# A third buffer for the low parts of q and k, taken from GpSimd's descriptor ring

## The chip, the core and the metric

The kernel runs on one core of a Trainium2 chip. The metric is the device time of one execution in microseconds (us), the median of several executions. The engines that matter are TensorE (PE, matmuls), VectorE (DVE), ScalarE (ACT), GpSimd (POOL) and SyncE (SP), which here only issues DMAs. Every engine has its own queue and works through it strictly in that order: an instruction that waits holds up all that stands behind it on its engine.

## What is computed

Causal attention over 8 batches, 8 heads, 576 tokens and head width 64, with a bias from a running sum; then a two-dimensional Fourier transform of the 512-wide tokens, added to them; then a layer norm and a two-layer MLP (512 to 2048 to 512). Cut to what matters:

```python
cum = np.cumsum(np.maximum(s, 0.0), axis=-1)
bias = -(cum[:, :, :, None] - cum[:, :, None, :])
scores = scale * np.matmul(q, k.transpose(0, 1, 3, 2))
scores = np.where(causal, -1e9, scores + np.minimum(bias, 0.0))
attn = np.exp(scores - scores.max(-1, keepdims=True))
attn = attn / (attn.sum(-1, keepdims=True) + 1e-09)
x = np.matmul(attn, v)                     # heads side by side: 8 x 576 x 512
u = x + np.real(np.fft.fft(np.fft.fft(x, axis=1), axis=2))
un = (u - mean(u)) / np.sqrt(var(u) + 1e-06)
out = u + np.maximum(un @ w_ch1, 0.0) @ w_ch2
```

## The kernel before

Attention goes by pairs of heads: 8 batches of 4 pairs make 32 pairs, and the main loop has 32 passes. Products are made in a reduced format in which a number is kept as a high part and a low part; three products of such parts stand for one exact one.

Pass i does these things side by side: `scores(i)` (L488, L489: the products of q and k for pair i, high parts from the tile KQ, low parts from q1 and k1; L492: the exponential on ACT into P), `maxes(i + 1)` (L456: products pm of the high parts; L463 on DVE: their row maxima into Mx; L468: Mx transposed on PE as pmt; L470 and L471: ACT copies it to mt and a DMA writes it into a row of KQ that scores(i + 1) reads), `low(i + 1)`, `high(i + 2)` (L415, L417: ACT copies q and k into KQ, one copy for each head) and `av(i - 1)` (L520: P times v). From pass 6 on, in every fourth pass and the one after it, `folds` runs on DVE, ACT and POOL (L250 to L265: Aw, Df, De, Do, e, eh, the even and odd halves that the Fourier products need), and `fourier` follows on PE (L283 to L314). MLP weights are converted beside it (L82 to L88). After pass 31 the MLP runs over all tokens.

`low(i)` is the part that the change touches. For a pair it issues two DMAs (L427, L428) that copy the high parts beside the low ones, two subtractions on DVE (L432, one for each head: k minus its high part, into k1) and two on POOL (L435, the same for q, into q1). q1 and k1 have two buffers, one in the pool `att` and one in the pool `atop`, by turns, so that pair i writes where pair i - 2 was read; scores(i - 2) ends with pass i - 2, and L432 of pair i stands at the start of pass i - 1.

KQ has three tiles (`NR = 3`, tile i % 3 for pair i), and the loaded inputs qk three buffers. The PE's order is written by hand (`weave` mixes the streams of a pass by their costs). The order on the other engines is set when the kernel is built, by a scheduler that puts an instruction where it believes it to be ready. `load_tables`, in pass 2, is the only place where GpSimd issues DMAs: nine, L233 to L237.

PSUM: pm and the products of `av` share five banks (`psm`), the products of scores and of Fourier share three (`ps`). A bank comes free when DVE (L463, L319, L320) or ACT (L492, L523 to L526) has read it.

Of the kernel before, what the change touches and what calls it, by code (L numbers as in the profile page):

```python
# [9 lines left out]
F32R = mybir.dt.float32r  # L10
# [6 lines left out]
PSUM = bass.MemoryType.PSUM  # L17
DRAM = bass.MemoryType.DRAM

S = 576  # L20
# [12 lines left out]

# key chunks: (keys, first query of the product, queries of the product, first query kept)
CH = [(128, 0, 576, 0), (128, 128, 448, 128), (128, 256, 320, 256), (128, 320, 256, 384), (64, 320, 256, 512)]
# [5 lines left out]
def fused_kernel(ctx, tc, qkT, vA, sP, wP, tabD, tabS, corr, out):  # L41
    nc = tc.nc
    NB = qkT.shape[0]
    NT = NB * S
    NP = NB * 4
# [8 lines left out]
    wD = dram.tile([NF, 128, 1024], F32, name="wD")  # L54
# [10 lines left out]

    # ---------------------------------------------------------------- MLP
    def split(dst_h, dst_l, src):
# [5 lines left out]
    def rounded(pool, f, x, bufs):  # L73
        """256 columns of chunk f of both weights, from the words of their float64, rounded to nearest: generates, returns the f32."""
        m = pool.tile([128, WC], I32, tag="wm", name="wm", bufs=bufs)
        raw = pool.tile([128, 2 * WC], I32, tag="raw", name="raw", bufs=bufs)
        nc.sync.dma_start(out=raw, in_=wP[f, :, WC * x:WC * x + WC].bitcast(I32))
        hi = raw.rearrange("p (n w) -> p n w", w=2)[:, :, 1]
        lo = raw.bitcast(U16).rearrange("p (n w) -> p n w", w=4)[:, :, 1]
        yield 0.0  # L80
        e = pool.tile([128, WC], I32, tag="we", name="we", bufs=bufs)
        nc.vector.tensor_scalar(e, hi, 0x7FF00000, None, op0=ALU.bitwise_and)  # L82
        nc.scalar.activation(e, e, AF.Relu, bias=wbias, scale=8.0)
        nc.vector.tensor_scalar(m, hi, 0xFFFFF, 0x100000, op0=ALU.bitwise_and, op1=ALU.bitwise_or)  # L84
        yield 0.4
        nc.vector.scalar_tensor_tensor(out=e, in0=hi, scalar=-0x80000000, in1=e, op0=ALU.bitwise_and, op1=ALU.bitwise_or)  # L86
        nc.vector.scalar_tensor_tensor(out=m.bitcast(F32), in0=lo, scalar=2.0 ** -16, in1=m, op0=ALU.mult, op1=ALU.add)  # L87
        nc.gpsimd.tensor_mul(e.bitcast(F32), m.bitcast(F32), e.bitcast(F32))  # L88
        yield 0.4
        return e.bitcast(F32)  # L90

    def convert_w(pool, lo, hi, bufs):
        """Chunks lo..hi-1 as f32, into wD."""
        for f in range(lo, hi):
            for x in range(1024 // WC):
                m = yield from rounded(pool, f, x, bufs)
                nc.sync.dma_start(out=wD[f, :, WC * x:WC * x + WC], in_=m)
                yield 0.2

    def load_w(pool, f):  # L100
        """Chunk f of both weights in high and low parts: into W."""
        wh = pool.tile([128, 1024], F32R, tag=f"wh{f}", name=f"wh{f}")
        wl = pool.tile([128, 1024], F32R, tag=f"wl{f}", name=f"wl{f}")
        W[f] = (wh, wl)
        if f < NC:
            nc.sync.dma_start(out=wl.bitcast(F32), in_=wD[f])
        n = 512 if f < NC else WC
        for x in range(1024 // n):
            xs = slice(n * x, n * x + n)
            m = wl[:, xs].bitcast(F32) if f < NC else (yield from rounded(stage, f, x, nstage))  # L110
            nc.scalar.copy(wh[:, xs], m)  # L111
            yield 0.2 * n / 512
            (nc.vector if x * n < 512 else nc.gpsimd).tensor_sub(wl[:, xs], m, wh[:, xs].bitcast(F32))  # L113
            yield 0.2 * n / 512

    def spread_sum(t, name, n):
        """1/512 of the sum of t over the partitions, on every partition (PSUM)."""
        th = lnp.tile([128, TOK], F32R, tag="th", name="th")
        tl = lnp.tile([128, TOK], F32R, tag="tl", name="tl")
        split(th[:, :n], tl[:, :n], t[:, :n])  # L120
        m = bank(name)
        nc.tensor.matmul(m[:, :n], ones, th[:, :n], start=True, stop=False)
        nc.tensor.matmul(m[:, :n], ones, tl[:, :n], start=False, stop=True)
        return m

    def ln_tile(t0, n, lag):
        """Centred tokens in high and low parts, their mean and 1 / deviation: generates into LN."""
        u = lnp.tile([128, 4, TOK], F32, tag="u", name="u")
# [32 lines left out]
    LN, W = {}, {}  # L161
# [51 lines left out]

    # ---------------------------------------------------------------- Fourier mixing
    fft_ctx = ExitStack()
# [27 lines left out]
    def folds(b, xa, xs):  # L243
        """The even and odd parts of one batch; xa: rows 0..255 of x^T, xs: rows 512-p and 384-p."""
        De = [fft.tile([128, 2, 289], F32R, tag=f"De{i}", name=f"De{i}") for i in range(2)]
# [27 lines left out]
    def fourier(b, xa, xs):  # L273
        """Fourier mixing of one batch in place."""
        De, Do = folded.pop(b)
# [66 lines left out]

    # ---------------------------------------------------------------- attention
    attb_ctx, att_ctx, atop_ctx = ExitStack(), ExitStack(), ExitStack()
# [4 lines left out]

    # Products of width 128: rows 0..2 carry the running sum (high, low) and the maximum,  # L350
    # rows 3..63 are zero, rows 64..127 carry the high parts of q and k.
    R = NB * NH
# [51 lines left out]
    def high(i):  # L404
        """The high parts of q and k, the running sums, and no maximum yet."""
        st = sts[i]
# [13 lines left out]
    def low(i):  # L420
        """The low parts of q and k, each beside the high part of the same."""
        st = sts[i]
        qk, qy, ky = st["qk"], st["qy"], st["ky"]
        pool = att if (NP - 1 - i) % 2 == 0 else atop
        q1 = pool.tile([128, 2, S], F32R, tag="q1", name="q1")
        k1 = pool.tile([128, 2, S], F32R, tag="k1", name="k1")
        nc.sync.dma_start(out=q1[0:64].bitcast(F32), in_=qy[64:128, :, 0:S].bitcast(F32))  # L427
# [75 lines left out]
    def av(i):  # L503
# [5 lines left out]
        for h in range(2):  # L509
            P = st["P"][h]  # L510
            vs = slice(64 * h, 64 * h + 128)
            for lo, n, tg in ((0, 256, "A"), (256, 320, "B")):
                p = psm.tile([128, 512], F32, tag="m", name="pav" + tg, bufs=5)
                cs = [c for c in range(5) if CH[c][3] < lo + n]
                for c in cs:
# [11 lines left out]
                    yield 4 * w / 2.4  # L527
            # the sums of P, the second head's beside a row of their own
            nc.sync.dma_start(out=sums[16 * h:16 * h + 16], in_=r1 if h else x[64:65])
# [90 lines left out]

    # ---------------------------------------------------------------- MLP over all tokens
    zp = ctx.enter_context(pool("zp"))
# [49 lines left out]
def take(gen, quota):  # L672
    """The part of a generator up to a cost."""
    done = 0.0
    while done < quota:
        try:
            c = next(gen)
        except StopIteration:
            return
        done += c  # L680
        yield c
# [17 lines left out]
def weave(*streams):  # L699
    """Runs generators side by side, each at the pace of its total cost."""  # L700
    for _ in mixed(*streams):
        pass
# [105 lines left out]
```

## Time and profile before

| | us |
|---|---|
| median of 3 runs | 1434.8 |
| lowest, highest | 1433.98, 1438.31 |
| the profiled execution's span | 1440.3 |
| PE busy in it | 1336.1 (93%) |
| DVE busy | 749.1 (52%) |
| ACT busy | 539.6 (37%) |
| POOL busy | 555.6 (39%) |

The first half of the span is attention and Fourier mixing, the second half the MLP. "Busy" does not count waiting. A wait is listed with the engine and line that waited and the engine and line that ended it.

### The profile page before, as it was taken

To read this page: it belongs to the slowest core of one execution; us is meant where nothing else is said; L and a number is where in the kernel's file an instruction comes from. 1 tells how busy PE (TensorE), PEld (TensorE's weight loads), DVE (VectorE), ACT (ScalarE), POOL (GpSimd) and SP (SyncE) were. 2 spreads that over 40 slices of the span, in tenths; PEclk is the share of its full clock that TensorE was granted. 3 is DMA by queue.
4 is the path that set the end of the run, shared out by engine and by line. 5 is a ranking of instruction groups with operands and counts; after the bars stand their busy time and mean duration, and the time that the engine had idled before them with its cause. 6 is when DMAs were issued, how large, how long until landed. Compare 5 with 4: busy or idle time off the path is not lost.

```text
span 1440.3 us, 17967 instructions
## 1 busy us (share of the span) xinstructions
PE 1336.1 (93%) x6190; PEld 1073.6 (75%) x6190; DVE 749.1 (52%) x1684; ACT 539.6 (37%) x1211; POOL 555.6 (39%) x540
## 2 busy tenths in 40 slices
PE   4987989897989897998799999999999999999998
PEld 2766767686867685786588888888888888888886
DVE  6667676867676778789833332133321323212212
ACT  4775656565656557344412121121211212112110
POOL 6454465655555566565641400314013140123300
PEclk9998989999989998899899999999999999999999
DMA  8655556565655545533200000000000000000000
GB/s 216 163 144 145 156 151 176 145 163 168 154 158 140 164 118 166 172 119 116 94 23 30 30 30 8 22 30 30 30 8 22 30 30 30 8 22 0 30 0 30
DMA packets 78166, 124.98 MB, mean 87 GB/s; under 512 B 11256, under 2 KB 36185, under 8 KB 78075
## 3 DMA queue, kind: packets, MB, share of 16 engines
q1 hardware_dynamic: 75627, 119.83, 28.8%
q0 software_dynamic: 1632, 2.43, 0.9%
q10 hardware_dynamic: 816, 1.57, 0.3%
q8 instruction: 49, 0.80, 0.2%
q14 instruction: 42, 0.34, 0.1%
HBM read 76.78 MB, written 23.07 MB: 69 GB/s over the span
## 4 chain that ended last, share of the span: by engine, by line
PE 50%; DVE 7%; POOL 2%; DMA 1%; issue 1%; ACT 1%; SPq 0%; DVEq 0%; POOLq 0%; ACTq 0%
PE h L182 25%; PE acc L197 8%; PE acc L195 8%; PE acc L196 8%; POOL we L88 1%; DVE wm L87 1%; DVE wm L84 1%; DVE we L82 1%; DVE wl L113 1%; DVE we L86 1%; DVE ucl L147 0%; DVE Df L259 0%; POOL wl L113 0%; DMA raw<-in_wP_dram 0%; ACT wh L111 0%
## 5 line engine op out<-in xcount | busy, mean ns | idle before, releaser
L187 DVE SCALAR_TENSOR_TENSOR zl<-h,zh 128x512 fp32r<-128x512 f32 x144 | 98.7, 686 | 405.6 <-ACT zh L186 405.6
L186 ACT ACTIVATE zh<-h 128x512 fp32r<-128x512 f32 x144 | 85.9, 596 | 531.7 <-PE h L182 531.7
L197 PE MATMUL acc<-zl,wh 128*128 128x512 f32 x576 | 227.5, 395 | 3.9 <-DVE zl L187 3.9
L195 PE MATMUL acc<-zh,wh 128*128 128x512 f32 x576 | 227.8, 396 | 1.2 <-ACT zh L186 1.2
L196 PE MATMUL acc<-zh,wl 128*128 128x512 f32 x576 | 226.9, 394 | 0.0
L520 PE MATMUL pavB<-P,va 128*128 128x320 f32 (+2 forms) x640 | 201.7, 404 | 7.8 <-ACT stage L524 7.1
L456 PE MATMUL pm<-KQ 128*128 128x256 f32 (+4 forms) x384 | 159.5, 434 | 38.5 <-DVE Mx L463 16.2
L492 ACT ACTIVATE P<-ps 128x320 f32<-128x320 f32 (+4 forms) x384 | 144.9, 390 | 116.7 <-PE ps L489 111.9
L488 PE MATMUL ps<-KQ 128*128 128x256 f32 (+3 forms) x384 | 153.0, 401 | 21.6 <-ACT P L492 12.8
L182 PE MATMUL h<-uch,wh 128*128 128x512 f32 x576 | 159.2, 397 | 8.3 <-ACT wh L111 8.3
L182 PE MATMUL h<-uch,wl 128*128 128x512 f32 x576 | 157.9, 396 | 0.8 <-DVE wl L113 0.8
L182 PE MATMUL h<-ucl,wh 128*128 128x512 f32 x576 | 157.2, 394 | 0.0
L463 DVE CUSTOM_DVE_ANT_0 trash<-pm,amask 128x128 bf16<-128x128 f32 (+3 forms) x256 | 123.8, 484 | 39.8 <-PE pm L456 23.3
L211 POOL TENSOR_TENSOR o<-o,w 128x512 f32<-128x512 f32 x32 | 41.6, 1301 | 251.6 <-issue 217.8
L182 PEld LDWEIGHTS h<-uch,wh 128*128 128x128 f32 x576 | 107.8, 189 | 35.8 <-ACT wh L111 11.9
L197 PEld LDWEIGHTS acc<-zl,wh 128*128 128x128 f32 x576 | 108.8, 189 | 30.9 <-DVE zl L187 5.8
L520 PEld LDWEIGHTS pavB<-P,va 128*128 128x128 f32 (+1 forms) x640 | 107.5, 198 | 32.4 <-issue 12.5
L182 PEld LDWEIGHTS h<-uch,wl 128*128 128x128 f32 x576 | 108.7, 189 | 26.6 <-DVE wl L113 1.5
L195 PEld LDWEIGHTS acc<-zh,wh 128*128 128x128 f32 x576 | 108.7, 189 | 26.4 <-ACT zh L186 2.1
L182 PEld LDWEIGHTS h<-ucl,wh 128*128 128x128 f32 x576 | 108.9, 189 | 24.7
L196 PEld LDWEIGHTS acc<-zh,wl 128*128 128x128 f32 x576 | 108.8, 189 | 24.8
L489 PE MATMUL ps<-q,k 128*128 128x256 f32 (+3 forms) x384 | 120.9, 317 | 1.4 <-POOL q L435 1.4
(139 smaller groups left out, 2035.1 us busy)
## 6 DMA issues: line engine op xcount, KB each, us to landing
qk<-in_qkT_dram SPq DMA_DIRECT2D x32, 576.0 KB
raw<-in_wP_dram SPq DMA_DIRECT2D x64, 256.0 KB
va<-in_vA_dram SPq DMA_DIRECT2D x32, 480.0 KB
q<-KQ SPq DMA_DIRECT2D x32, 288.0 KB
k<-KQ SPq DMA_DIRECT2D x32, 288.0 KB
rb<-rd SPq DMA_DIRECT2D x64, 144.0 KB
u<-uD SPq DMA_DIRECT2D x8, 1024.0 KB
out_dram<-o SPq DMA_DIRECT2D x32, 256.0 KB
```

The source lines that it names most:

```text
L182: nc.tensor.matmul(h[:, :n], a[:, j * 128:(j + 1) * 128], b[:, j, :n], start=i == 0, stop=i == 11)
L186: nc.scalar.activation(zh[:, :n], h[:, :n], AF.Relu)
L187: nc.vector.scalar_tensor_tensor(out=zl[:, :n], in0=h[:, :n], scalar=0.0, in1=zh[:, :n].bitcast(F32), op0=ALU.max, op1=ALU.subtract)
L195: nc.tensor.matmul(acc[j][:, :n], a[:, cs], y[:, :n], start=g == 0, stop=False)
L196: nc.tensor.matmul(acc[j][:, :n], b[:, cs], y[:, :n], start=False, stop=False)
L197: nc.tensor.matmul(acc[j][:, :n], a[:, cs], z[:, :n], start=False, stop=g == NF - 1)
L456: nc.tensor.matmul(p[:nq, :n], qy[:, h, 128 * c:128 * c + nq], ky[:, h, k0:k0 + n], start=True, stop=True)
L463: nc.vector.tensor_tensor_reduce(out=trash[:nq, :n], in0=p[:nq, :n], in1=amask[:nq, m0:m0 + n], scale=1.0, scalar=first if x else NEG, op0 ...
L488: nc.tensor.matmul(p[:nk, :n], ky[:, h, ksl], qy[:, h, a:a + n], start=True, stop=False)
L489: nc.tensor.matmul(p[:nk, :n], k1[:, h, ksl], q1[:, h, a:a + n], start=False, stop=True)
L492: nc.scalar.activation(P[:nk, o:o + a + n - lo], p[:nk, lo - a:n], AF.Exp, scale=0.125)
L520: nc.tensor.matmul(p[:, a - lo:n], va[:nk, c, vs], P[:nk, o:o + w], start=c == 0, stop=c == cs[-1])
```

## The change

q1 and k1 get three buffers instead of two: pairs with (31 - i) % 3 = 0 use one buffer in `att`, the others two buffers in `atop` in turn. The room, 9 KB in each partition, comes from the area that holds the descriptors of GpSimd's DMAs, which is made 4 KB in each partition in place of 16 KB. Some comments are dropped, too.

```diff
     def low(i):
-        pool = att if (NP - 1 - i) % 2 == 0 else atop
-        q1 = pool.tile([128, 2, S], F32R, tag="q1", name="q1")
-        k1 = pool.tile([128, 2, S], F32R, tag="k1", name="k1")
+        pool, bufs = (att, 1) if (NP - 1 - i) % 3 == 0 else (atop, 2)
+        q1 = pool.tile([128, 2, S], F32R, tag="q1", name="q1", bufs=bufs)
+        k1 = pool.tile([128, 2, S], F32R, tag="k1", name="k1", bufs=bufs)
...
-    nc = bacc.Bacc("TRN2", target_bir_lowering=False, num_devices=1)
+    nc = bacc.Bacc("TRN2", target_bir_lowering=False, num_devices=1, dynamic_dma_scratch_size=4096)
```

The SP queue stays the same, and so does the PE's but for one swap in pass 0. The order on DVE changes, and in two stretches that on ACT and POOL. In the rows below, k_987 is the tile of low parts of pair 6, k_1144 that of pair 7, k_2126 of pair 12, k_2336 of pair 13 and k_3720 of pair 20; "x2" means both heads in a row; L463 comes as two rows, the maximum and the reading of it.

On DVE at the start of pass 5 (the difference, + is new):

```order
 L463 ISA Mx_126 64x1
 L432 TENSOR_TENSOR k_987<-qk,KQ_119 64x576 x2
+L432 TENSOR_TENSOR k_1144<-qk,KQ_120 64x576 x2
 L463 ISA trash,Mx_125<-pm,amask 128x128
 L463 ISA Mx_125 128x1
```

Pair 7 moves up from the start of pass 6 to that of pass 5. In the same way pair 8 moves from the start of pass 7 to that of pass 6. This repeats with a period of three passes: one place that holds two pairs, one that holds the next pair but one in place of its own, one that holds none. On DVE at the start of pass 19, within the folds (the difference):

```order
 L255 TENSOR_TENSOR Df<-Aw 128x289
 L320 TENSOR_TENSOR yp<-yc,pys 128x290
-L432 TENSOR_TENSOR k_3720<-qk,KQ_121 64x576
+L265 TENSOR_TENSOR eh<-e,eh 1x289
 L69 TENSOR_TENSOR De_3538<-Df,De_3537 128x289
-L265 TENSOR_TENSOR eh<-e,eh 1x289
 L259 TENSOR_TENSOR Df<-Bw 128x288
-L432 TENSOR_TENSOR k_3720<-qk,KQ_121 64x576
 L69 TENSOR_TENSOR Do_3540<-Df,Do_3539 128x288
 L463 ISA trash,Mx_125<-pm,amask 128x128
```

This is a place that holds none now: both subtractions of pair 20 are gone from it, a pass ahead. On DVE from the end of pass 10 into pass 11, before:

```order
L265 TENSOR_TENSOR eh<-e,eh 1x289
L319 TENSOR_TENSOR ym<-yc,pys 128x290
L69 TENSOR_TENSOR Do_1942<-Df,Do_1941 128x288
L320 TENSOR_TENSOR yp<-yc,pys 128x290
L255 TENSOR_TENSOR Df<-Aw 128x289
L432 TENSOR_TENSOR k_2126<-qk,KQ_119 64x576 x2
L69 TENSOR_TENSOR De_1940<-Df,De_1939 128x289
L259 TENSOR_TENSOR Df<-Bw 128x288
L463 ISA trash,Mx_125<-pm,amask 128x128
```

The same stretch now:

```order
L432 TENSOR_TENSOR k_2126<-qk,KQ_119 64x576
L259 TENSOR_TENSOR Df<-Bw 128x288
L319 TENSOR_TENSOR ym<-yc,pys 128x290
L320 TENSOR_TENSOR yp<-yc,pys 128x290
L69 TENSOR_TENSOR Do_1942<-Df,Do_1941 128x288
L265 TENSOR_TENSOR eh<-e,eh 1x289
L255 TENSOR_TENSOR Df<-Aw 128x289
L432 TENSOR_TENSOR k_2336<-qk,KQ_120 64x576 x2
L69 TENSOR_TENSOR De_1940<-Df,De_1939 128x289
L463 ISA trash,Mx_125<-pm,amask 128x128
```

Here pair 12 moved up within the folds (its other head stands six rows further up, behind L250), pair 13 took its old place, and the second L259 moved behind L463. Pass 22 to 23 (pairs 24 and 25) has the same shape.

## Rows read from the trace of the kernel before

**Rows 1.** Windows: stretch, length, busy us of each engine (instructions), granted clock, DMA.

```profile
72.00:144.00 72.00, 60.10 (x283) 46.18 (x282) 49.47 (x131) 46.01 (x112) 35.84 (x37) 0.86 0.55 144
...
288.00:360.00 72.00, 64.27 (x352) 52.01 (x351) 52.24 (x158) 44.84 (x111) 38.71 (x42) 0.95 0.58 166
...
720.00:1440.00 720.00, 714.64 (x3098) 581.14 (x3096) 207.74 (x271) 125.66 (x213) 153.22 (x114) 1.00 0.06 22
```

**Rows 2.** Waits: engine, line <- what ended them: us, times, longest.

```profile
DVE k L432 <- PE ps L489: 58.7, 20, 5.5
...
PE pm L456 <- DVE Mx L463: 16.2, 9, 5.0
...
PE ps L488 <- ACT P L492: 12.8, 11, 2.2
...
DVE k L432 <- ACT P L492: 6.8, 2, 4.1
...
PE pmt L468 <- DVE Mx L463: 3.4, 3, 2.4
```

**Rows 3.** Line 432: count, ns shortest/median/longest, first and last start.

```profile
L432 DVE TENSOR_TENSOR k<-qk,KQ x64: 749/1182/1970, 7.7 to 525.5; 64x576 fp32r<-64x576 f32 x64
```

**Rows 4.** Timeline, start of pass 18: start, us, engine, instruction, [idle before <- releaser].

```profile
312.90 1.86 DVE L432 TENSOR_TENSOR k<-qk,KQ 64x576 fp32r<-64x576 f32 x2 [4.34 <-PE ps L489]
313.02 0.67 ACT L415 CAST KQ<-qk 64x576 fp32r<-64x576 f32 x1
...
314.88 0.29 DVE L463 CUSTOM_DVE_ANT_0 trash<-pm,amask 128x128 bf16<-128x128 f32 x1
...
315.88 0.42 PE L456 MATMUL pm<-KQ 128*128 128x384 f32 x1
```

**Rows 5.** Timeline of PE, passes 0 to 2.

```profile
19.95 0.38 PE L468 MATMUL pmt<-ident,Mx 128*10 128x128 f32 x1 [2.39 <-DVE Mx L463]
...
36.77 0.55 PE L488 MATMUL ps<-KQ 128*128 128x256 f32 x1 [3.70 <-DMA KQ<-mt]
...
46.66 0.27 PE L468 MATMUL pmt<-ident,Mx 128*10 128x128 f32 x1
```

**Rows 6.** Timeline of PE, start of pass 4.

```profile
80.45 1.44 PE L520 MATMUL pavB<-P,va 128*128 128x320 f32 x2 [0.55 <-ACT stage L524]
```

**Rows 7.** Timeline, end of pass 10 and start of pass 11.

```profile
191.18 0.43 ACT L68 CAST Do<-Df 128x288 fp32r<-128x288 f32 x1 [1.48 <-DVE Df L259]
...
192.00 0.33 PE L488 MATMUL ps<-KQ 128*64 128x256 f32 x1 [2.22 <-ACT P L492]
...
194.22 2.34 DVE L432 TENSOR_TENSOR k<-qk,KQ 64x576 fp32r<-64x576 f32 x2
...
198.76 0.69 PE L456 MATMUL pm<-KQ 128*128 128x384 f32 x1 [3.22 <-DVE Mx L463]
```

**Rows 8.** Timeline, start of pass 19.

```profile
332.00 0.87 DVE L432 TENSOR_TENSOR k<-qk,KQ 64x576 fp32r<-64x576 f32 x1
...
335.64 1.44 DVE L432 TENSOR_TENSOR k<-qk,KQ 64x576 fp32r<-64x576 f32 x1
...
337.84 0.69 PE L456 MATMUL pm<-KQ 128*128 128x384 f32 x1 [5.03 <-DVE Mx L463]
```

**Rows 9.** Timeline of PE, end of pass 22 and start of pass 23.

```profile
400.34 0.34 PE L488 MATMUL ps<-KQ 128*64 128x256 f32 x1 [2.21 <-ACT P L492]
...
406.88 0.69 PE L456 MATMUL pm<-KQ 128*128 128x384 f32 x1 [0.76 <-DVE Mx L463]
```

**Rows 10.** Windows of 4 us in pass 11, columns as in rows 1.

```profile
196.00:200.00 4.00, 0.69 (x1) 0.28 (x1) 3.54 (x9) 0.69 (x2) 2.59 (x3) 0.50 0.46 177
...
204.00:208.00 4.00, 4.00 (x26) 3.33 (x24) 3.10 (x13) 1.64 (x5) 0.87 (x2) 1.00 0.99 267
```

**Rows 11.** GpSimd's DMA queue (packets, MB, share), and POOL behind its nine issues.

```profile
q0 software_dynamic: 1632, 2.43, 0.9%
...
28.30 2.78 POOL L435 TENSOR_TENSOR q<-qk,q 64x576 fp32r<-64x576 f32 x2 [3.09 <-DMA q<-KQ]
```

## The prediction

> **What bounds the kernel now.** First the windows [rows 1]. In the MLP half PE is busy 714.64 of 720.00 us: PE alone sets the time there, and the change touches nothing of it. In the attention half PE is busy 60.10 and 64.27 of 72 us, DVE 46.18 and 52.01. PE is still the fullest engine, but waits for 8 to 12 us in every 72, so this half is set by PE's work plus its own waits. A change of DVE's order counts only where it shortens or lengthens a wait of PE.
>
> Next the waits by engine [rows 2]. The largest wait at the touched line is DVE's: L432 waits 58.7 us, 20 times, for the end of the products of scores, and 6.8 us, 2 times, for an exponential: 65.5 us together. This is what a third buffer should remove. But it is DVE's wait. PE's waits that DVE ends are far smaller: 16.2 us in 9 times for Mx at pm and 3.4 at pmt, together 19.6. Nothing more than this can come back from a faster DVE.
>
> Then the timeline at an ordinary pass boundary, pass 18 [rows 4]. DVE waits 4.34 us for the last products of scores, subtracts for 1.86 us in two rows, and begins L463 at 314.88. PE's product pm that follows starts at 315.88, and its row names no wait. So DVE's wait is slack: the products of `scores`, `maxes` and `av` fill PE in the meantime.
>
> **The third buffer, place by place.** What happens to the 65.5 us? The order on DVE moves with a period of three passes. One place holds two pairs, the next holds the pair after its own, the third holds none. With three buffers pair m needs the end of scores(m - 3) instead of scores(m - 2). A pair hoisted by one pass, to the start of pass m - 2, stands exactly where scores(m - 3) ends: it waits for the same event as the pair whose place it took. So the wait stays at two of three places and goes only at the third: about 65.5 / 3 = 22 us of DVE's waiting disappear, and the number of subtractions stays at 64 [rows 3]. The change does half of what it says, and where it does it the wait was mostly slack.
>
> What is left is the few places where PE stands close behind DVE. In passes 0 to 2 the new pairs are hoisted into work that PE waits for; in the folds the chain DVE to ACT to DVE is tight.
>
> *Pass 0.* The two subtractions of pair 2 move ahead of the last maxima of pass 0, so ahead of pmt at 19.95, which already waits 2.39 us for DVE [rows 5]. Their price is the shortest of line 432, 0.75 us each [rows 3], since neither folds nor `av` work beside them yet: 2 x 0.75 = 1.5. The other end is 0: PE waits 3.70 us for a DMA at 36.77 in any case [rows 5], and a delay before it is swallowed as far as that DMA does not itself come out of the delayed pmt. Bounds 0 and +1.5; I take the middle, +0.7.
>
> *Pass 1.* Pair 3 moves ahead of the maxima that pmt at 46.66 reads; there is no wait in that row now [rows 5], so there is some cover, of unknown size. From 0 to two subtractions of some 0.94 us (about half way from shortest to median, rows 3), +1.9; I take +1.0.
>
> *Pass 4.* Its place holds none now. PE waits 0.55 us for ACT's `stage` at 80.45 [rows 6], with DVE shortly behind: bounds -0.75 (a subtraction of the shortest kind) and 0; I take -0.5.
>
> *Passes 10 and 11* (pairs 12 and 13). Pair 12's two subtractions stand inside the folds now, ahead of Df and so of ACT's Do (191.18, which already waits 1.48 us for Df); pair 13's are where pair 12's were, 2.34 us in a row [rows 7]. PE waits 3.22 us for Mx at 198.76 behind these. For it: one L259 moved behind Mx, worth about 0.86 us. Also, on ACT the exponential moves ahead of Do, so PE's wait of 2.22 us at 192.00 [rows 7] shrinks; against it, PE then meets ym and yp later. Best case -1.0; worst, the two inserted subtractions fully on the path, +2.3 (2.34, rows 7). I take +0.8, above the middle, since the existing wait of 3.22 says that DVE is already late.
>
> *Pass 19.* Here the gain is. Pair 20's subtractions, 0.87 and 1.44 us, vanish from a chain behind which PE waits 5.03 us at 337.84 [rows 8]: 0.87 + 1.44 = 2.3 at most. Part of DVE's chain here waits for ACT between its steps, which hides some of the first one: I take -1.8, bounds -2.3 and 0.
>
> *Passes 22 and 23* (pairs 24 and 25) have the same shape as 10 and 11: PE waits 2.21 us at 400.34 for the exponential and only 0.76 us at 406.88 for Mx [rows 9]. Less is late here: +0.5, bounds -1.0 and +2.3.
>
> *All other places* cost nothing: a second pair at a place takes two subtractions of about 1.2 us [rows 3] out of slack such as the 4.34 us of rows 4, and the place without a pair gives back slack. If that cover is gone, it is a matter of up to 2.4 us at each such place.
>
> A stall has a second price. In the 4 us of the stall in pass 11 PE's granted clock is 0.50, the lower level (1.2 GHz), and at 204 to 208 it is 1.00 again [rows 10]. Each stall removed or made longer may thus move some work between the two levels; its size is in rival B.
>
> **The descriptor ring.** GpSimd's queue carries 1632 packets and 0.9% of the time of 16 engines [rows 11], in nine issues of pass 2. POOL's next instruction, L435 at 28.30, waits 3.09 us for a DMA of q, not for these issues. I take 0; the bound is rival D.
>
> The Trainium skill, page "DMA: Bandwidth & Descriptors", sections "Terms" and "SWDGE vs HWDGE vs iDMA", says that a descriptor takes 16 bytes and that GpSimd's rings lie in a part of SBUF set aside for them. An estimate from that page: 4096 / 16 = 256 descriptors against 1632 / 16 = 102 packets for each engine [rows 11], so the ring would not fill. No run here shows a full ring.
>
> **The sum.** +0.7 + 1.0 - 0.5 + 0.8 - 1.8 + 0.5 = +0.7 us. The profiled execution's span is 1440.3, so 1441.0 there; the median of the three runs is 1434.8, which is 5.5 lower, and on it the forecast is 1435.5. The sum of all lower bounds is -0.75 - 1.0 - 2.3 - 1.0 = -5.05, of the upper ones 1.5 + 1.9 + 2.3 + 2.3 = +8.0: 1429.8 to 1442.8. All at one end is unlikely; the forecast's own range is 1431 to 1440.
>
> **Rivals.**
>
> *A, faster.* DVE's 22 us of freed time reach PE. The stalls of pm and pmt behind Mx, 16.2 + 3.4 = 19.6 us [rows 2], shrink: wholly gone 1415, by half 1425. For it: DVE is ahead by a pass at one place in three, and everything behind it may start earlier. Against it: of PE's large waits only those at 198.76 and 337.84 have L432 ahead of them at all [rows 7, 8], and at the first it stays. It decides if PE's waits for Mx in passes 11, 19 and 23 all fall below 1 us.
>
> *B, slower.* The pairs hoisted into tight places cost their upper bounds: +1.5 + 1.9 + 2.3 + 2.3, with -0.5 and -1.8 where places are empty, = +5.7. A longer stall also keeps PE at 1.2 GHz for longer [rows 10]: half of the clock over a further 2 to 3 us of work is about +1 to +1.5. Together about +7, so 1442. For it: an inserted subtraction in the folds can take up to 1.97 us instead of the median 1.18 [rows 3], and POOL's folds and subtractions run beside it. Against it: the ACT swap gives PE its bank earlier. It decides, as slower, from a sum of +4.3 on: passes 11 and 23 have to lose some 2 us each, and the early passes their upper bounds.
>
> The Trainium skill, page "SBUF — State Buffer", section "Who interferes with whom", says that a VectorE instruction with two inputs in SBUF contends with a GpSimd instruction that reads SBUF, and that the order of issue decides which of them is held up. The trace agrees so far as the same subtraction takes 749 to 1970 ns [rows 3]. An estimate by that page, if DVE is always the one held up: the four subtractions of pairs 12 and 24 take 1.97 in place of the 1.17 that 2.34 / 2 gives [rows 7], 3.2 more than in my sum, so 1438.7.
>
> *C, no change at all in the mechanism.* The wait at L432 keeps two thirds, and PE's stalls fall where they fell: that is my forecast with all place terms at zero, 1434.8.
>
> *D, the ring.* With a quarter of the space POOL has to wait during its nine issues until earlier ones have landed, and L435 behind them (2.78 us in two rows [rows 11]) is late, with q1 of pair 3 and scores behind it. One such wait as long as its present 3.09, wholly on the path, gives 1438.6, two of them 1441.7. For it: POOL's L435 follows right behind. Against it: the queue is busy for only 0.9% [rows 11].
>
> **How the numbers follow.** Forecast and C together 0.65, A 0.15, B 0.17, D 0.03. A measurement of this kernel can tell about 0.3% from no change, 4.3 us: 1430.5 to 1439.1 counts as the same. Faster takes A and 0.02 of the forecast's lower tail: 0.17. Slower takes B and D: 0.20. The rest, 0.63, is the same. The range goes from 1429 (below the sum of lower bounds; it leaves out most of A, about 0.12) to 1443 (the sum of upper bounds; it leaves out some 0.05 of B). Cases of one sign do not hold most of the chance; the likeliest has its own range above.
>
> **What would show it.** In the changed kernel's list of waits DVE's at L432 should fall from 65.5 us to about 44, in some two thirds of the times, still ended by PE at L489 (or by ACT's copies right behind it). PE's wait for Mx in pass 19 (5.03 now) should be near 3; those in passes 11 and 23 (3.22 and 0.76) the same or up to 2 longer, those for exponentials (2.22, 2.21) shorter; pmt in pass 0 (2.39) up to 1.5 later. PE's busy time in the MLP should stay. If L432 hardly waits any more, my reading of the period of three is wrong; if it hardly waits and the time falls by over 4.3, DVE's waiting was not slack. If PE's waits at pm grow by 2 or more at several places, it is B. If POOL shows a new wait behind its nine issues, it is D. The forecast is wrong above all if cover that I took as ample (rows 4) is used up at the places with two pairs.

## The result and the profile after

| | before | after |
|---|---|---|
| median, us (11 runs each) | 1435.63 | 1439.08 |
| lowest to highest, us | 1432.65 to 1438.31 | 1436.92 to 1442.94 |
| ratio after / before | | 1.0036, 95% interval 1.0022 to 1.0049 |
| span of the traced execution, us | 1440.3 | 1436.6 |

By the ratio the change makes the kernel slower by 0.36%, about 5.2 us; the two medians differ by 3.5 us. The forecast was +0.7 us and "no change" as the likeliest case. The time lies in the range, on the side that rival B described, and at the edge of what was called the same: by the median just inside (1439.08 against 1439.1), by the ratio just outside (0.36% against about 0.3%).

The two traced executions say the opposite of the medians: the slower kernel's trace is 3.7 us shorter. A second trace of the kernel before, taken later, had a span of 1430.9 us, 9.4 less than the first with the same program. Of these 9.4 us, 8.3 are PE's busy time (1336.1 against 1327.8 us), at a mean granted clock of 0.962 against 0.969; only 1.1 are waiting of PE. So the spans of two traces decide nothing here. What decides is the repeated timing, and, inside the traces, the length of single passes against its scatter: some repeat to 0.1 us, those of the table below to 1 or 2 us.

Two windows of the kernel after (columns as in rows 1):

```profile
288.00:360.00 72.00, 65.17 (x354) 52.39 (x353) 55.48 (x158) 45.07 (x111) 41.55 (x42) 0.95 0.59 172
720.00:1440.00 720.00, 711.00 (x3082) 578.15 (x3080) 207.82 (x271) 123.85 (x211) 149.31 (x113) 1.00 0.06 22
```

The picture of [rows 1] is unchanged: PE full in the MLP, and waiting for some 7 us of 72 in the attention half. The waits of the kernel after (engine, line <- what ended them: us, times, longest; "issue" is a wait for nothing that the profile shows):

```profile
DVE trash L463 <- PE pm L456: 64.2, 44, 6.5
PE pm L456 <- DVE Mx L463: 18.9, 12, 6.2
DVE k L432 <- ACT P L492: 17.7, 7, 4.3
PE ps L488 <- ACT P L492: 15.8, 14, 3.7
DVE k L432 <- issue: 11.4, 3, 4.4
DVE k L432 <- PE ps L489: 6.5, 4, 4.2
PE pmt L468 <- DVE Mx L463: 6.3, 4, 4.4
DVE k L432 <- ACT KQ L415: 2.7, 4, 0.9
```

and the one row of the kernel before that [rows 2] left out:

```profile
DVE trash L463 <- PE pm L456: 27.8, 43, 4.4
```

DVE's wait at L432 fell from 67.3 us (58.7 + 6.8 + 1.8) to 38.3 (17.7 + 11.4 + 6.5 + 2.7). In the same step DVE's next wait, for PE's products pm at L463, grew from 27.8 to 64.2. DVE got no time back: it stands idle one instruction later. PE's waits for DVE did not shrink: 16.2 to 18.9 at pm, 3.4 to 6.3 at pmt. At pm that is no more than scatter: two further traces of the order before, before_again and ring_only (see the experiments), have 15.2 and 19.3; at pmt both have 3.7.

**Pass 11**, where the largest loss is. Timeline of DVE, POOL and PE in the kernel after (start, us, engine, instruction, [idle before <- releaser]):

```profile
187.22 1.86 DVE L432 TENSOR_TENSOR k<-qk,KQ 64x576 fp32r<-64x576 f32 x1
192.16 0.75 DVE L432 TENSOR_TENSOR k<-qk,KQ 64x576 fp32r<-64x576 f32 x1
197.09 3.61 DVE L432 TENSOR_TENSOR k<-qk,KQ 64x576 fp32r<-64x576 f32 x2
201.10 0.28 DVE L463 CUSTOM_DVE_ANT_0 trash<-pm,amask 128x128 bf16<-128x128 f32 x1
...
186.65 3.70 POOL L435 TENSOR_TENSOR q<-qk,q 64x576 fp32r<-64x576 f32 x2
197.12 0.79 POOL L322 TENSOR_TENSOR xa<-xa,yp 128x287 f32<-128x287 f32 x1
197.87 0.79 POOL L323 TENSOR_TENSOR xs<-xs,yp 128x289 f32<-128x289 f32 x1
198.62 0.78 POOL L324 TENSOR_TENSOR xs<-xs,ym 128x287 f32<-128x287 f32 x1
...
201.45 0.69 PE L456 MATMUL pm<-KQ 128*128 128x384 f32 x1 [6.15 <-DVE Mx L463]
```

In [rows 7] PE waited 3.22 us there and pair 12's two subtractions took 2.34. Now pair 12's two take 1.86 + 0.75 in the folds, pair 13's two 3.61 behind them (2.94 and 0.75, overlapping a little), and PE waits 6.15. Over seven traces of the order before (named under "The lengths of passes") this wait is 1.85 to 4.01 us, in the second trace of the changed kernel 5.51. The long subtractions lie beside POOL's L435 and beside its three additions in a row, which the new order put together (before, an instruction of L495 stood between two of them). The same in pass 23, where pair 25's two stand apart, so that each shows its length:

```profile
405.23 2.95 DVE L432 TENSOR_TENSOR k<-qk,KQ 64x576 fp32r<-64x576 f32 x1
410.41 0.75 DVE L432 TENSOR_TENSOR k<-qk,KQ 64x576 fp32r<-64x576 f32 x1
...
405.27 0.79 POOL L322 TENSOR_TENSOR xa<-xa,yp 128x287 f32<-128x287 f32 x1
406.02 0.80 POOL L323 TENSOR_TENSOR xs<-xs,yp 128x289 f32<-128x289 f32 x1
406.78 0.79 POOL L324 TENSOR_TENSOR xs<-xs,ym 128x287 f32<-128x287 f32 x1
```

It takes 2.95 us beside the three additions, which end at 407.57, and 0.75 where POOL does nothing. Line 432 as a whole in the kernel after (count, ns shortest/median/longest):

```profile
L432 DVE TENSOR_TENSOR k<-qk,KQ x64: 748/789/2952, 7.7 to 507.6; 64x576 fp32r<-64x576 f32 x64
```

The longest is 2952 ns, against 1970 in [rows 3]. PE's clock behind the stall, in windows of 4 us:

```profile
198.00:202.00 4.00, 0.55 (x1) 0.29 (x1) 3.97 (x8) 0.20 (x1) 1.40 (x2) 0.54 0.79 295
202.00:206.00 4.00, 3.05 (x8) 2.23 (x8) 2.96 (x11) 2.58 (x8) 2.10 (x2) 0.50 0.89 279
206.00:210.00 4.00, 4.00 (x17) 3.15 (x17) 2.52 (x12) 1.04 (x3) 0.15 (x1) 0.68 0.60 146
```

PE had the lower level (1.2 GHz) as in [rows 10] while it stood and when its work resumed; over the last 4 us it had 0.68, where [rows 10] end with 1.00.

**Passes 19 and 22 to 23**, PE in the kernel after:

```profile
338.11 0.55 PE L456 MATMUL pm<-KQ 128*128 128x384 f32 x1 [2.77 <-DVE Mx L463]
...
399.81 0.33 PE L488 MATMUL ps<-KQ 128*64 128x256 f32 x1 [1.72 <-ACT P L492]
402.30 1.66 PE L335 MATMUL p<-scos,z 97*4 97x290 f32 x9 [1.71 <-ACT P L492]
...
409.65 0.69 PE L456 MATMUL pm<-KQ 128*128 128x384 f32 x1 [2.12 <-DVE Mx L463]
```

The wait of 5.03 us in [rows 8] is 2.77; all seven traces of the order before have 5.02 to 5.04 there, so this is the change. The one of 0.76 in [rows 9] is 2.12, in the second trace of the changed kernel 1.43, and this shows nothing: with the order before it is 0.76 to 0.88 in three traces and 2.60 or 2.61 in four, such as ring_only:

```profile
401.50 0.44 PE L456 MATMUL pm<-KQ 128*128 128x384 f32 x1 [2.60 <-DVE Mx L463]
```

New in pass 22 is PE's wait of 1.71 us for an exponential at L335. The one for an exponential at L488, 2.21 in [rows 9], is shorter, 1.72, as forecast.

**The lengths of passes.** To separate the change from the scatter between executions, the table takes the time from the first product of scores of a pass to that of the next, from PE's timeline. "Order before" are the seven traces of kernels with the order of before in these passes (before twice, and the experiments ring_only, pair2_only, pair3_only, early_only, early_again): their mean, and how far single ones lie from it. The other columns are differences from that mean, in us; after has two traces.

| pass | order before: mean | scatter | after | folds_only | one_input | fold_free |
|---|---|---|---|---|---|---|
| 6 | 17.27 | -0.94 to +0.47 | -1.15, -1.35 | -1.06 | -0.08 | +0.24 |
| 10 | 18.13 | -0.85 to +1.18 | -1.35, 0.00 | -0.20 | +0.60 | +1.52 |
| 11 | 19.82 | -0.88 to +1.02 | +3.05, +3.24 | +2.37 | -0.21 | -2.65 |
| 12 | 16.09 | -0.58 to +1.07 | -0.21, +0.65 | +2.18 | +2.95 | +1.69 |
| 19 | 21.41 | -0.43 to +0.30 | -1.20, -1.87 | -0.62 | -1.54 | -2.07 |
| 22 | 19.19 | -0.67 to +1.25 | +1.37, +1.71 | +1.78 | -0.55 | +1.43 |
| 23 | 17.89 | -0.60 to +0.40 | +1.61, -0.05 | -0.09 | +2.57 | -3.87 |
| 10 and 11 together | 37.95 | -0.55 to +1.05 | +1.70, +3.24 | +2.16 | +0.40 | -1.13 |
| 22 and 23 together | 37.08 | -0.29 to +0.65 | +2.98, +1.66 | +1.69 | +2.02 | -2.43 |

The scatter column understates what one trace can do: folds_only has the order of before in pass 6 and is 1.06 shorter there, and the order of the change in pass 12 and is 2.18 longer, where the changed kernel is not. How much of these lengths is PE's waiting (length less busy time, us; seven traces of the order before):

| | order before | after | folds_only | one_input | fold_free |
|---|---|---|---|---|---|
| pass 11 | 3.10 to 5.26 | 7.10, 6.46 | 6.26 | 4.05 | 2.05 |
| pass 19 | 5.96 to 5.98 | 4.45, 4.31 | 5.97 | 4.31 | 4.31 |
| passes 22 and 23 | 4.14 to 6.60 | 6.50, 5.71 | 5.77 | 7.24 | 2.79 |
| span's start to pass 31 | 71.9 to 77.0 | 73.1, 73.5 | 80.0 | 79.2 | 71.4 |

In passes 11 and 19 the change is one of waiting. In passes 22 and 23 it is not: the changed kernel waits as long there as kernels with the order before. Nor does it wait longer in sum up to pass 31. What is longer in its two traces is PE's busy time over this stretch, 469.4 and 471.1 us at a granted clock of 0.94, against 460.2 to 465.0 at 0.95 to 0.96 in six traces of the order before; but the seventh has 469.9 at 0.93, and over the timed runs of after_again the mean clock is 0.968, against 0.969 for the kernel before beside it. So whether the change brings a lower clock is not shown.

### The profile page after: what moved, and what is told of

Its sections match the earlier page's. It is cut to its first block, busy times and chain, and to the rows that moved or that the text cites. A ratio compares the mean times of both kernels' runs of the same rounds, so it can differ in the third digit from the quotient of the medians.

```text
span 1436.6 us, 17960 instructions
## 1 busy us (share of the span) xinstructions
PE 1333.6 (93%) x6190; PEld 1072.2 (75%) x6190; DVE 746.5 (52%) x1684; ACT 540.7 (38%) x1211; POOL 550.9 (38%) x540
## 3 DMA queue, kind: packets, MB, share of 16 engines
q0 software_dynamic: 1632, 2.43, 0.8%
## 4 chain that ended last, share of the span: by engine, by line
PE 50%; DVE 7%; POOL 2%; DMA 1%; issue 1%; ACT 1%; SPq 0%; DVEq 0%; POOLq 0%; ACTq 0%
PE h L182 25%; PE acc L195 8%; PE acc L197 8%; PE acc L196 8%; POOL we L88 1%; DVE we L82 1%; DVE wm L87 1%; DVE wl L113 1%; DVE wm L84 1%; DVE we L86 1%; DVE Df L259 0%; POOL wl L113 0%; DMA raw<-in_wP_dram 0%; ACT wh L111 0%; DVE ucl L147 0%
## 5 line engine op out<-in xcount | busy, mean ns | idle before, releaser
L456 PE MATMUL pm<-KQ 128*128 128x256 f32 (+4 forms) x384 | 159.6, 434 | 38.7 <-DVE Mx L463 18.9
L488 PE MATMUL ps<-KQ 128*128 128x256 f32 (+3 forms) x384 | 155.0, 406 | 22.7 <-ACT P L492 15.8
L463 DVE CUSTOM_DVE_ANT_0 trash<-pm,amask 128x128 bf16<-128x128 f32 (+3 forms) x256 | 123.6, 483 | 76.4 <-PE pm L456 60.0
```

Source lines behind the costliest of these rows:

```text
L456: nc.tensor.matmul(p[:nq, :n], qy[:, h, 128 * c:128 * c + nq], ky[:, h, k0:k0 + n], start=True, stop=True)
L463: nc.vector.tensor_tensor_reduce(out=trash[:nq, :n], in0=p[:nq, :n], in1=amask[:nq, m0:m0 + n], scale=1.0, scalar=first if x else NEG, op0 ...
L488: nc.tensor.matmul(p[:nk, :n], ky[:, h, ksl], qy[:, h, a:a + n], start=True, stop=False)
```

## The experiments

Theory E: the moves in passes 0 and 1 are the loss. Theory F: the two places where two pairs now stand in the folds (passes 10 to 11 and 22 to 23) are most of it. Besides: the ring, and rival A, that DVE's freed time is worth something. In the expectations "theory 1" is E and "theory 2" is F.

**The kernel before again, and the ring alone** (two buffers; no instruction moves):

```diff
-    nc = bacc.Bacc("TRN2", target_bir_lowering=False, num_devices=1)
+    nc = bacc.Bacc("TRN2", target_bir_lowering=False, num_devices=1, dynamic_dma_scratch_size=4096)
```

> The kernel before, once more, against itself. Both theories: ratio 1.000, within 0.0015. Its trace gives a second look at the same order: where its TensorE instructions start differently from the first trace, by up to some 4 us, the difference is one between executions and not one of a kernel.

> The kernel before with two buffers for the low parts and only the descriptor area cut from 16 KB to 4 KB. Order theory: no instruction moves, so ratio 1.000 (1434 to 1437 us). Ring theory: GpSimd waits between its nine table DMAs or the last ones land later, and the whole loss of about 0.36% shows here (about 1440.8 us).

Measured: 0.9994 (0.9980 to 1.0007) and 1.0011 (0.9988 to 1.0034). The times cannot exclude a third of a per cent for the ring; POOL's rows show no wait that it could come from. Of ring_only:

```profile
24.92 0.53 POOL L237 DMA_DIRECT2D cor<-in_corr_dram  x1
28.46 2.80 POOL L435 TENSOR_TENSOR q<-qk,q 64x576 fp32r<-64x576 f32 x2 [3.02 <-DMA q<-KQ]
```

The nine issues stand where they stood, two at 10.32 to 12.00 us and seven without a gap from 21.23 on; the last takes 0.53 us as before, and L435 waits 3.02 us where it waited 3.09 [rows 11]. This L435 is pair 1's, not pair 3's as rival D had it. In the changed kernel it does wait longer, 4.70 us, but in pair2_only, where only pair 2 moves early, it waits 4.38: that goes with the early move, not with the ring. Rival D is out.

**The early moves.** The third buffer serves pair 1 and the last pair only, so that pairs 2 and 3 move as in the change and pairs 4 to 30 stay:

```diff
-        pool, bufs = (att, 1) if (NP - 1 - i) % 3 == 0 else (atop, 2)
+        pool, bufs = (att, 1) if i in (1, NP - 1) else (atop, 2)
```

> The changed kernel, but with a third buffer that is used only by pair 1 (and the last pair), so that pairs 2 and 3 have their subtractions moved up into the maxima of passes 0 and 1 as in the changed kernel, and pairs 4 to 30 have them where they stood before. Theory 1 (the moves in passes 0 and 1 are the loss, and the later ones about cancel): 3.5 to 6 us slower than before, ratio 1.0025 to 1.004. Theory 2 (the moves in the folds, passes 10 and 22 above all, are the loss; the early delay is swallowed by the wait for KQ<-mt at 36.77): within 1 us of before, ratio 0.9995 to 1.001.

> The kernel with only the early moves, once more, for a narrower interval. Theory E: ratio 1.0025 to 1.004. Theory F: the early moves carry the smaller part, ratio 1.000 to 1.002.

Measured: 1.0009 (0.9990 to 1.0028), and again 1.0012 (0.9994 to 1.0031). Some 1.5 us at the best guess, and both intervals include no change. Theory E, which wanted 1.0025 or more, is not borne out, though each interval alone just reaches that far. Each move alone, for one look at the first 100 us (slots: which buffer a pair takes, C is the one in `att`):

```diff
+        slot = "ACB"[i] if i < 3 else "BC"[i % 2]              # pair 2 alone
+        slot = "C" if i in (1, NP - 1) else "AB"[i % 2]        # pair 3 alone
```

> The order before, but for pair 2, whose two subtractions are moved up into the maxima of pass 0. Read in the trace up to 100 us. Theory 1a (the wait for KQ<-mt at 36.77 swallows this delay): pmt near 20 us about 2 us later, and nothing left of it from 40 us on (within 1 us). Rival (mt comes out of the delayed pmt, so the delay stays): 2 us later from there to 100 us.

> The order before, but for pair 3, whose two subtractions are moved up into the maxima of pass 1 (and the last pair, which has the third buffer). Theory 1b (this move is the early loss): nothing up to 40 us, then 3.5 to 5.5 us later at 60 us, and so at 100 us. Rival (only the subtractions' own time counts): 1.9 us later at 60 us.

PE in pair2_only:

```profile
21.30 0.38 PE L468 MATMUL pmt<-ident,Mx 128*10 128x128 f32 x1 [2.38 <-DVE Mx L463]
...
36.97 0.36 PE L488 MATMUL ps<-KQ 128*128 128x256 f32 x1 [2.68 <-DMA KQ<-mt]
```

pmt comes 1.35 us later than in [rows 5], and at 36.97 against 36.77 us the delay is gone: the DMA of mt swallowed it. (In the changed kernel pmt comes 2.04 us later, at 21.99; its two subtractions take 0.75 and 1.25 us there, the longer one beside POOL's L435.) With pair 3 alone PE stays within 0.5 us of the range of before, before_again and ring_only over these 100 us, so neither expectation for it came true. (Alone its two subtractions took 0.75 us each, in the change 1.07 and 0.85.) The early part costs little; at the start of pass 4 the two traces of the changed kernel were 3.8 and 0.1 us behind the latest of these three, so it also scatters.

**The later moves without the early ones.** Pairs 2 and 3 stay, every pair from 4 on moves up by one pass (one pair at each place, unlike in the change; the tiles have names of their own here, and the scheduler placed the work otherwise):

```diff
+        slot = "ABAB"[i] if i < 4 else "BCA"[i % 3]
```

> Three buffers, but pairs 2 and 3 write where pairs 0 and 1 were read, so that their subtractions stand where they stood before; from pair 4 on each pair has the third buffer and is moved up by one pass. Theory 1: no slower than before, ratio 0.997 to 1.000. Theory 2: the loss is here, ratio 1.002 to 1.004.

Measured: 1.0011 (0.9991 to 1.0031), inconclusive between the two. It has a third buffer, no pair standing doubly in the folds, and shows no gain: 0.1% at most. DVE's wait at L432 is 70.3 us in its trace, no shorter than the 67.3 of before. That fits the forecast's reading that a pair which takes its predecessor's place waits as that one did.

**Is DVE's time worth anything?** late3, and from pair 5 on the subtraction covers 8 of 576 columns, so most of the low part of k is left out of the product; the three k1 tiles are also kept from pair to pair. Of the edit:

```diff
-            nc.vector.tensor_sub(k1[0:64, h], qk[64:128, h], ky[64:128, h].bitcast(F32))
+            (... if i < 5 else nc.vector.tensor_sub(k1[0:64, h, 0:8], qk[64:128, h, 0:8], ky[64:128, h, 0:8].bitcast(F32)))
```

> Three buffers with pairs 2 and 3 where they stood before, and from pair 5 on the subtraction for k is made over 8 of 576 columns only, so the low part of k is left out in most of the product: neither the work nor the wait of line 432 is left for these pairs (about 50 us of DVE's work and 60 of its waiting). Theory (DVE's time there is slack): ratio 0.996 to 1.001. Rival A (DVE's freed time reaches TensorE): 8 to 20 us faster, ratio 0.986 to 0.9945.

Measured: 0.9971 (0.9955 to 0.9987), 4.2 us faster than before, against late3 some 5.7; 8 to 20 us against the kernel before are excluded. DVE was busy for 713.1 us instead of 749.1. The wait did not go away as I had written: it moved to the copies of the high parts:

```profile
DVE k L432 <- ACT KQ L415: 83.2, 36, 5.9
```

So 36 us less of DVE's work is worth some 4 to 6 us. What the waiting ahead of it is worth this run does not test, since the wait stayed.

**The changed kernel again.**

> The changed kernel once more. If its loss is 0.36% it repeats: ratio 1.002 to 1.005. If the first comparison was partly scatter between executions (the kernel before spreads over 13 us here), it comes nearer to 1.001. Its trace should again show TensorE's pmt of pass 0 some 2.1 us later than before, and by 60 us into the span a delay of 4 to 6 us.

Measured: 1.0039 (1.0022 to 1.0055). The loss repeats; a delay of 4 to 6 us at 60 us did not (see above).

**The folds alone.** The third buffer serves five pairs, which gives passes 8 to 13 and 20 to 25 the order of the change:

```diff
-        pool, bufs = (att, 1) if (NP - 1 - i) % 3 == 0 else (atop, 2)
+        pool, bufs = (att, 1) if i in (10, 13, 22, 25, NP - 1) else (atop, 2)
```

> The third buffer is used only by pairs 10, 13, 22, 25 and 31, so that the stretches of passes 8 to 13 and 20 to 25 (the folds of passes 10 and 22 among them) stand on VectorE, ScalarE and GpSimd as in the changed kernel, and the other places as before (pair 1's subtractions move up into pass 0, a delay that the wait for KQ<-mt swallowed where pair 2 was moved alone). Theory F (the two places where two pairs stand in the folds are most of the loss): TensorE loses about 3.3 us in pass 11 and 1 to 3 us over passes 22 and 23 against the runs in the order before, ratio 1.002 to 1.0045. Theory E (the early moves are the loss): pass 11 differs by under 1 us, ratio 0.999 to 1.001.

Measured: 1.0026 (1.0006 to 1.0046), and in the table +2.37 in pass 11 and +1.78 in pass 22. Theory F holds: with little more than these two places moved, the loss is 3.7 us (0.9 to 6.6) of the 5.2, though pass 12 adds 2.18 to this trace and not to the changed kernel's. PE waits in pass 11 as in the changed kernel:

```profile
204.37 0.69 PE L456 MATMUL pm<-KQ 128*128 128x384 f32 x1 [5.31 <-DVE Mx L463]
```

**One input in place of two** for the four pairs concerned, in the changed kernel:

```diff
+            (nc.vector.tensor_scalar(out=k1[0:64, h], in0=ky[64:128, h].bitcast(F32), scalar1=0.0, scalar2=None, op0=ALU.mult) if i in (12, 13, 24, 25) else ...
```

> The changed kernel, but for pairs 12, 13, 24 and 25 line 432 writes its high part times zero (one input) in place of the difference of two, so the low part of k is left out for these four pairs; the instructions stand where they stood in passes 10 to 11 and 22 to 23. In the changed kernel pair 13's two took 3.61 us in pass 11 beside three additions on GpSimd, and one took 2.95. Theory P (an instruction with two inputs is held up while GpSimd adds beside it): pair 13's two take 1.6 us or less, TensorE's wait for Mx in pass 11 falls from 5.5 to 6.2 us to some 3.5 to 4.2, and the ratio to 1.000 to 1.002. Rival (any instruction of this size is slow there, or the inserted order is the loss): 3 us or more for the two, the wait stays above 5 us, ratio 1.003 to 1.005.

Timeline of DVE and PE in it:

```profile
188.17 1.56 DVE L432 TENSOR_SCALAR k<-KQ 64x576 fp32r<-64x576 f32 x1
192.81 0.46 DVE L432 TENSOR_SCALAR k<-KQ 64x576 fp32r<-64x576 f32 x1
197.60 1.74 DVE L432 TENSOR_SCALAR k<-KQ 64x576 fp32r<-64x576 f32 x2
...
201.34 0.69 PE L456 MATMUL pm<-KQ 128*128 128x384 f32 x1 [2.80 <-DVE Mx L463]
```

Pair 13's two take 1.74 us instead of 3.61 (1.6 or less was expected), PE's wait falls to 2.80, which is within the 1.85 to 4.01 of the order before, and pass 11 is as long as before the change (-0.21). The ratio, 1.0020 (1.0005 to 1.0034), is the upper end of what was expected, and its interval overlaps the changed kernel's: that the kernel became faster is not shown. Passes 10 to 12 together are as long as in the changed kernel (+3.3 us against +1.5 and +3.9), with a wait of PE of 2.22 us for an exponential in pass 12, and so are passes 22 and 23, where PE waits 3.65 us for Mx although the subtractions are short.

The test is not clean either: with one input the instruction is shorter in itself (0.46 against 0.75 where nothing holds it up), beside POOL's L435 it took 1.56 too, and the order on POOL and ACT differs in the stretch (L323 and L324 no longer stand next to each other). It agrees with the reading that the length of these instructions makes PE's wait in pass 11, and that they are long where POOL works beside them. How much hangs on the second input it does not separate, and for passes 22 and 23 it speaks against this reading.

**Out of the folds.** If subtractions in the folds cost, those that stood there before can leave. Three buffers, given out so that only pairs 8, 12, 16, 20, 24 and 28 move, to the end of the pass ahead:

```diff
-        pool, bufs = (att, 1) if (NP - 1 - i) % 3 == 0 else (atop, 2)
-        q1 = pool.tile([128, 2, S], F32R, tag="q1", name="q1", bufs=bufs)
-        k1 = pool.tile([128, 2, S], F32R, tag="k1", name="k1", bufs=bufs)
+        slot = "C" if i % 2 else "A" if i < 8 else "BA"[i // 4 % 2]
+        q1 = (att if slot == "C" else atop).tile([128, 2, S], F32R, tag="q1" + slot, name="q1")
+        k1 = (att if slot == "C" else atop).tile([128, 2, S], F32R, tag="k1" + slot, name="k1")
```

> Three buffers given out so that only the pairs whose subtractions stood in the tail of the folds (8, 12, 16, 20, 24, 28) are moved, to the start of the pass ahead, outside the folds; all others, the early ones too, stay. Theory F: each emptied place gives up to what pass 19 gave in the changed kernel (1.3 to 1.9 us), those whose stall was ended by something else nothing: 2 to 6 us faster, ratio 0.996 to 0.9985, and nothing lost at the places with two pairs. Rival (the stalls in the folds are ended by other work in any case): ratio 0.9995 to 1.001.

Measured: 1430.03 us, ratio 0.9957 (0.9938 to 0.9976): faster than before by 6.2 us, a little more than the 2 to 6 expected. PE and the waits of it:

```profile
199.26 0.44 PE L456 MATMUL pm<-KQ 128*128 128x384 f32 x1 [0.91 <-DVE Mx L463]
```

```profile
DVE k L432 <- PE ps L489: 51.3, 20, 5.4
PE pm L456 <- DVE Mx L463: 9.2, 9, 2.8
```

DVE waits at L432 for 51.3 us, nearly as long as in the kernel before (58.7), and the kernel is faster: PE's wait for Mx is 9.2, against 15.2 to 19.3 in before, before_again and ring_only. The gain is larger than small3's, although small3 has less work. In the table passes 11, 19 and 23 gave 2.65, 2.07 and 3.87, and passes 12 and 22 gave back 1.69 and 1.43; the other three emptied places, in passes 7, 15 and 27, gave -0.26, -0.27 and +0.15, nothing beyond scatter. These are lengths from one trace: it reaches pass 31 at 536.6 us, where these three reach it at 535.8 to 544.4, so the gain itself rests on the timing.

## Why the prediction was right, and where not

- **The main reading held.** DVE's wait was slack. It was taken off at L432 by 29 us and came back at L463 by 36. The wait fell somewhat more than the 65.5 to 44 that was forecast; this gained nothing for PE. Rival A is excluded by the time itself, and by PE's waits for Mx, which did not shrink; small3 adds that even 36 us less of DVE's work is not worth what A wanted.
- **Pass 19** was right in place and size: -1.8 forecast, -1.2 and -1.9 in the two traces, of which PE's waiting is -1.5 and -1.7.
- **The ring** cost nothing that the rows show, as forecast. The Trainium skill's page "DMA: Bandwidth & Descriptors", sections "Terms" and "SWDGE vs HWDGE vs iDMA", from which 256 descriptors against 102 had been estimated, agrees with this; the estimate counted one descriptor for each packet, where the section names a pair for each operation, which would make 204, still below 256. A full ring was not seen.
- **Passes 10 to 11** are the step that failed. The place was named, the term was mis-sized: +0.8 with bounds -1.0 and +2.3, measured +1.7 and +3.2 over both passes (pass 11 alone +3.1 and +3.2; in pass 10 the wait for the exponential shrank, as forecast), and +2.2 in folds_only. The bound priced two more subtractions at the 2.34 us they had taken there before. It left open that pair 13's would be put beside three additions of POOL and take 3.61 (in pass 23, 2.95 the one of them beside POOL). Rival B named just this (long subtractions beside POOL) but capped one at the 1.97 of the kernel before, which is the longest of that order and no bound for another.
- **Passes 22 to 23**: +0.5 forecast with bounds -1.0 and +2.3, +3.0 and +1.7 measured. The long subtraction stands here too, but PE does not wait longer than with the order before, so why these passes are longer stays open.
- **Passes 0 and 1**: +1.7 forecast, 1.3 and 1.7 us measured by early_only and early_again, with intervals from below nothing to 4.5 us. The DMA at 36.77 swallowed pass 0's part, of which half had been charged. Its two subtractions took 0.75 and 1.25 us, not 0.75 each, as POOL's L435 ran beside the second.
- **Pass 4**: -0.5 forecast, -0.5 and +0.7 in the traces, within scatter.

The terms as measured, -1.5 for pass 19, +2.5 for passes 10 and 11, +2.3 for passes 22 and 23, +1.5 for the early passes, make +4.8; the timing says +5.2 by the ratio, +3.5 by the medians. The agreement is better than the scatter of the terms warrants. Pass 6 (-1.2) is not in it; folds_only, with the order of before there, has -1.06. That the time fell into the range was partly luck: two terms came out near their upper bounds or above, and pass 19 paid for part of it.

The rule of the Trainium skill, page "SBUF — State Buffer", section "Who interferes with whom", pointed the right way: a VectorE instruction with two inputs in SBUF contends with GpSimd's reads, and the estimate by it, +3.9 us in all, was nearer than the sum. The traces agree: 0.75 us alone and 2.95 beside three GpSimd additions; that one_input's TENSOR_SCALAR also took 1.56 in place of 0.46 beside GpSimd fits what the section says of `tensor_scalar` where that runs in a mode with two ports, but no run here shows which mode it was in. That the estimate came near is partly luck: of the subtractions that it put at 1.97 us each, pair 12's took 1.86 and 0.75, and the longest was one of pair 13's.

Open: why passes 22 and 23 are longer; why passes 12 and 23 differ among kernels that have the same order there (in pass 12 the long ones, folds_only, one_input, fold_free and late3, have a wait of PE for an exponential of 1.44, 2.22, 0.97 and 2.59 us, the others at most 0.35); and whether the change brings PE a lower clock.

## What to carry to other kernels

A third buffer removes a wait, but the waiting engine then stops at its next input; look first whether the bounding engine waits for it at all. A scheduler uses new freedom to move work, and moved work has the price of its new neighbours, not of its old row: bound it by what the engine beside it does there. A single trace's wait is not yet an effect: compare it with several traces of the old order first. Give the freedom only to the instructions that stand in somebody's way: the same memory spent on six pairs gained 0.43%, spent on all pairs it lost 0.36%.

## What was not expected of the hardware

One and the same subtraction, 64x576 words, took 0.75 us alone and 2.95 us beside three additions on GpSimd of 0.79, 0.80 and 0.79 us: about their sum and its own time. And one program on one core scattered by 13 us between executions (1429.69 to 1442.63 us over 35 runs of the kernel before), more than most effects studied here, while single passes of it, such as pass 18, repeated to 0.01 us.
